# One place modulo 512 bytes for the tiles that TensorE streams, and six operands a pair, not eight, in the inverse transform over k1

## The chip, the cores and the metric

The kernel runs on one core of one Trainium2 chip. The metric is the device time of one execution in microseconds (us); it is given as the median of several executions. Engines are named as in the profile: PE is TensorE's matmul, PEld its weight load, DVE is VectorE, ACT is ScalarE, POOL is GpSimd, SP is SyncE, which here only issues transfers.

## The reference

```python
# attention part, B = 2, S = 12480, D = 128
h_filt = np.maximum(pos_emb @ w1, 0.0) @ w2 * exp(-0.01 * pos)
y = irfft(rfft(x * v, 2 * S) * rfft(h_filt, 2 * S))[:, :S]      # a long convolution per channel
x1 = (x * y).reshape(24960, 128)
# first layer of experts, d_ff = 2048
h = x1 @ w_in
x2 = (h * clip(h + 3, 0, 6) / 6) @ w_out
# second layer
h = maximum(x2 @ w_in2, 0)
out = (h * h) @ w_out2
```

All data are float32. The kernel writes a float32 number as a high and a low part of the type float32r, and makes a product of float32 accuracy from three matmuls of float32r (high by low, low by high, high by high). A matmul whose operands are float32 is made of two instructions.

## The kernel before, in words

**The convolution.** The first stretch makes the filter and, for 32 groups of four channels, the forward transforms, the products and the inverse transform over one of the two indices (`s1`, `s2`, `s3`). `keep` copies what comes out into a staging tile `stg` for a block of 16 channels of both sequences, and `write` sends each of the eight blocks to two tensors in DRAM, `zda` (the first ZA = 4 pairs) and `zdb` (the other 60).

**The pairs.** What is left of the inverse transform is a sum over k1 (K1 = 90 values, real and imaginary part, so 180 rows), for 64 pairs of positions j. `tile_loads` brings for a pair its two halves `za`, `zb`, the table `vt` and the factor `xt`, each with three buffers. `combine` adds and subtracts the two halves to `pp` and `pn` (VectorE for j < 3, then GpSimd). `s4` multiplies: for each of `pp`, `pn` and each of the two sequences two matmuls of 90 rows and 98 (97) columns, one for the real and one for the imaginary part, eight a pair, into one PSUM bank, 390 tokens in all. `gate` multiplies with `xt`, `gate_high` and `gate_low` make the high and the low part `oh`, `ol`.

**The experts.** The 24960 tokens go through both layers in 49 tiles: one of 390 tokens, 47 of 512 and one of 506. A tile of a layer is eight steps. A step is `l1` (two chunks of 128 hidden units, three matmuls each, streaming `oh`, `ol` in layer 1 and `xh`, `xl` in layer 2 into the PSUM tile `ph`), `relu`, `act` and `split` on ScalarE, VectorE and either VectorE or GpSimd (they make `gh` and `gl`), and, LAG = 3 steps later, `l2` (six matmuls that stream `gh`, `gl` into `acc`): 12 matmuls of 512 columns. The weights are `wp0` to `wp3`.

**The order** is written out by hand: what the program issues first on an engine runs first there. The list `tiles` has 15 tiles of layer 1, then one of layer 2 and one of layer 1 in turn, and the rest of layer 2 at the end (AHEAD = 14). The pairs' matmuls are put between those of the steps by `between`, which each step calls at four places:

```python
for f, args, rate in begun.pop(n, ()) if place == 0 else ():
    filling["s4"] = f(*args), rate
if "s4" in filling:
    turn, rate = filling["s4"]
    for _ in range(rate or place % 2):
        if "s4" in filling and next(turn, True):
            del filling["s4"]
```

At rate 2 (19 pairs, those of the first 15 tiles) each place takes two matmuls of a pair, at rate 1 (10 pairs) one, at rate 0 (34 pairs) every second place takes one. What is put in at one place is called a piece below. `gate` and what follows it are planned at the step `done`, and the loads of pair j behind the gate of pair j - 3.

**The start of the experts.** Pair 0 is loaded while the convolution ends, and its last block comes straight from `stg`. Then SP issues `loads(1)`, `loads(2)`, the last `zdb` write and `loads(3)` in this order. A DMA from SP or ACT counts on one of eight semaphores in turn, and waits until the DMA that used the same one before has landed.

Of the kernel before, what the change touches and what calls it, by code (L numbers as in the profile page):

```python
# [37 lines left out]

LEAST = 1.125 * 2.0 ** -15
UOFF = [(0, 98), (98, 98), (196, 97), (293, 97)]  # L40


@with_exitstack
def tile_hyena_moe(ctx: ExitStack, tc, xg, vg, xT, pos, w1d, w2d, fmat, fwin, twc,
                   tws, twcf, twsf, dcs, inv, vtab, w_in1, w_out1, w_in2, w_out2, out):
# [7 lines left out]
    zds = [tc.dram_tile([2, ZA, NBLK, K1, 64], F32, name="zda"),  # L53
           tc.dram_tile([2, 64 - ZA, NBLK, K1, 64], F32, name="zdb")]


    three = cp.tile([128, 1], F32, name="three")


    early = ctx.enter_context(ExitStack())  # L60
# [83 lines left out]
    xv = early.enter_context(tc.tile_pool(name="xv", bufs=3))  # L144
    us = {}
# [113 lines left out]
    def keep(i):  # L259
        g, s = divmod(i, 3)  # L260
        blk, ch0 = g // 4, (g % 4) * 4
        ps = ps3s.pop(i)
        if blk not in stg:
            stg[blk] = sp.tile([128, K1, 2, 2, 16], F32, name=f"stg{blk}", tag="stg")
        nc.scalar.activation(
            stg[blk][:, :, :, s - 1, ch0:ch0 + 4].rearrange("p k r c -> p r c k"),
            ps[:, :, :K4].rearrange("p r (c k) -> p r c k", c=4), AF.Copy)
        if g % 4 == 3 and s == 2:
            sv = stg.pop(blk).rearrange("p k r b c -> p k (r b c)")
            if blk == NBLK - 1:  # L270

                for h, t in enumerate((za, zb)):
                    nc.scalar.dma_start(t.rearrange("k d r b c -> k d (r b c)")[:, blk], sv[64 * h:64 * h + 1])
# [101 lines left out]
    with tc.tile_pool(name="cv_ps", bufs=4, space=PSUM) as vps:  # L375
        def write(blk, z, sv, queue=nc.scalar):
            lo, hi = ((0, ZA), (ZA, 64))[z]
            for h in range(2):
                queue.dma_start(zds[z][h, :, blk], sv[64 * h + lo:64 * h + hi])

        tail, late_rows = [], []
        s1(0)
        twiddle(0)
        s2(1)
        s1(3)
        split1(0)
        twiddle(3)
        s2(2)
        product(1, 0)
        product(1, 1)  # L390
        load(2, 0)
        load(2, 1)
        for i in range(NI + 2):

            a, z = i + AH, i - 2
            if i < NI and i not in (1, 2):
                s2(i)
            if 3 < a < NI:
# [74 lines left out]
    LAG = 3  # L473

    def loads(j):
        za = mo.tile([K1, NBLK, 2, 2, 16], F32, name=f"za{j}", tag="za", bufs=3)
        zb = mo.tile([K1, NBLK, 2, 2, 16], F32, name=f"zb{j}", tag="zb", bufs=3)
        vt[j] = mo.tile([K1, 2, 2, N1], F32, name=f"vt{j}", tag="vt", bufs=3)
        xt[j] = mo.tile([128, TOK], F32, name=f"xt{j}", tag="xt", bufs=3)
        tile_loads(j, za, zb, vt[j], xt[j])  # L480
        zt[j] = (za, zb)

    def combine(j):

        za, zb = zt.pop(j)
        pp = mo.tile([K1, 2, 2, D], F32, name=f"pp{j}", tag="pp")
        pn = mo.tile([K1, 2, 2, D], F32, name=f"pn{j}", tag="pn")
        pm[j] = (pp, pn)

        p, n = (t.rearrange("k r b (d c) -> k d r b c", d=NBLK) for t in (pp, pn))  # L490
        if j == 0:
            for t, z in ((p, za), (n, zb)):
                for r in range(2):
                    nc.scalar.activation(t[:, :, r], z[:, :, r], AF.Copy)
                yield
            return
        for k in range(2):
            for r in range(2):
                eng = nc.vector if j < 3 else nc.gpsimd
                eng.tensor_tensor((p, n)[k][:, :, r], za[:, :, r], zb[:, :, 1 - r],  # L500
                                        (ALU.add, ALU.subtract)[k])
            yield

    py = {}
# [1 line left out]
    def bank(name, k):  # L506
        return mps.tile([128, 512], F32, name=name, tag=f"acc{k % 2}", bufs=1)

    def s4(j, k):

        ps = bank(f"py{j}", k)
        v = vt.pop(j)
        for u in range(4):
            q, b = divmod(u, 2)
            o, n = UOFF[u]
            for r in range(2):
                nc.tensor.matmul(ps[:, o:o + n], pm[j][q][:, r, b, :],  # L517
                                 v[:, q, r, :n], start=(r == 0), stop=(r == 1))
                if u == 3 and r == 1:
                    pm.pop(j)  # L520
                    py[j] = ps
                yield
# [33 lines left out]
    for t in range(1, NTI):  # L556
# [63 lines left out]
    def relu(n):  # L620
        w = size[steps[n][1]]
        r = mo.tile([128, 2, TM], F32, name=f"r{n}", tag="r", bufs=4)
        if steps[n][0] == 0:
            nc.scalar.activation(r[:, :, :w], ph[n][:, :, :w], AF.Relu, bias=three)  # L624
        else:
            nc.scalar.activation(r[:, :, :w], ph[n][:, :, :w], AF.Relu)  # L626
        rs[n] = r
# [72 lines left out]
    for turn in (combine(0), s4(0, 1)):  # L700
        for _ in turn:
            pass
    decode(1, 1)
    decode(2, 1)
    decode(0, 3)
# [45 lines left out]
def _tables():  # L751
# [24 lines left out]
    f = lambda z: np.ascontiguousarray(z, dtype=np.float32)  # L776
    return dict(fmat=f(fmat), fwin=f(fmat * wa), twc=f(twc), tws=f(tws),
                twcf=f(twc * wb[:, None]), twsf=f(tws * wb[:, None]),
                dcs=f(dcs), inv=f(inv), vtab=f(vtab))


def _token_index():
# [59 lines left out]
```

## Time and profile before

| | us |
|---|---|
| median of three runs (2772.34 to 2773.39) | 2772.64 |
| profiled execution, device time | 2773.49 |
| profiled execution, span of the core | 2771.5 |
| TensorE busy | 2728.0 |
| VectorE busy | 1999.9 |
| ScalarE busy | 1932.0 |
| GpSimd busy | 1594.2 |

The profiled execution is 0.85 us over the median. The span falls into three stretches: the convolution (to about 471 us), layer 1 alone with the decoding of layer 2's weights (to about 845 us), and then tiles of both layers in turn, of layer 2 alone at the end. The profile models the end of a matmul: a matmul is listed with its time from first to last element, which overlaps the next one's. What a matmul costs is read from one start to the next.

### The profile page before, as it was taken

What the parts mean: (1) busy time and instruction counts of PE and PEld (TensorE: products, weight loads), DVE (VectorE), ACT (ScalarE), POOL (GpSimd) and SP (SyncE); (2) the same over time, 40 slices, a digit from 0 to 9 for tenths busy, and PEclk for the clock granted to TensorE, in tenths of its full rate; (3) what the DMA queues carried; (4) which work ended last, traced back from release to release, by engine and by line L of the source; (5) the groups of instructions that cost most, each with busy time, mean ns of one, the idle gap of its engine ahead of it and who ended that gap; (6) DMA issues with size and microseconds to landing.
All of it is one profiled execution on the core that took longest, in us unless ns stands there. A gap on an engine that the chain in (4) does not pass through costs nothing.

```text
span 2771.5 us, 33774 instructions
## 1 busy us (share of the span) xinstructions
PE 2728.0 (98%) x12862; PEld 2281.0 (82%) x12862; DVE 1999.9 (72%) x1976; ACT 1932.0 (70%) x2192; POOL 1594.2 (58%) x884
## 2 busy tenths in 40 slices
PE   7999999999999999999999999999999999999999
PEld 6899998788888888888888888888888888888887
DVE  6898998998976666666666666666666666666666
ACT  5445545677777777777777777777777777777776
POOL 3888885576665555555545464645455554444444
PEclk9999999999999999999999999999999999999999
DMA  3253544311111001111010010010111110000000
GB/s 121 80 166 112 146 112 117 99 47 58 40 42 35 18 25 26 27 25 29 25 28 25 21 33 20 24 29 25 29 25 29 25 29 5 8 8 12 12 12 16
DMA packets 136463, 122.28 MB, mean 44 GB/s; under 512 B 99370, under 2 KB 114798, under 8 KB 134894
## 3 DMA queue, kind: packets, MB, share of 16 engines
q1 hardware_dynamic: 127570, 86.27, 11.4%
q10 hardware_dynamic: 8732, 33.85, 4.5%
q8 instruction: 101, 1.65, 0.2%
q14 instruction: 60, 0.49, 0.1%
HBM read 83.68 MB, written 36.37 MB: 43 GB/s over the span
## 4 chain that ended last, share of the span: by engine, by line
PE 89%; DVE 6%; ACT 1%; issue 1%; POOL 0%; DMA 0%; POOLq 0%; ACTq 0%; DVEq 0%
PE ph L616 36%; PE acc L664 36%; PE p L225 7%; PE p L179 4%; PE py L517 3%; PE p L256 3%; DVE r L633 1%; DVE gl L647 1%; ACT gh L643 0%; ACT r L624 0%; DVE ol L542 0%; DVE wm L117 0%; DVE wa L114 0%; DVE wa L125 0%; DVE wa L108 0%
## 5 line engine op out<-in xcount | busy, mean ns | idle before, releaser
L647 POOL TENSOR_TENSOR gl<-r,gh 128x1024 fp32r<-128x1024 f32 (+2 forms) x401 | 966.9, 2411 | 1036.5 <-ACT gh L643 990.4
L664 PE MATMUL acc<-gh,wp 128*128 128x512 f32 (+2 forms) x3136 | 874.8, 399 | 7.5 <-DVE ol L542 7.5
L643 ACT ACTIVATE gh<-r 128x1024 fp32r<-128x1024 f32 (+2 forms) x784 | 820.0, 1046 | 21.1 <-DVE r L633 20.5
L633 DVE SCALAR_TENSOR_TENSOR r<-r,ph 128x1024 f32<-128x1024 f32 (+2 forms) x392 | 475.3, 1213 | 345.6 <-ACT r L624 345.1
L636 DVE SCALAR_TENSOR_TENSOR r<-ph,r 128x1024 f32<-128x1024 f32 (+2 forms) x392 | 477.9, 1219 | 341.9 <-ACT r L626 341.7
L664 PEld LDWEIGHTS acc<-gh,wp 128*128 128x128 f32 x3136 | 575.5, 188 | 123.2 <-PE ph L616 10.4
L624 ACT ACTIVATE r<-ph,three 128x1024 f32<-128x1024 f32 (+2 forms) x392 | 436.1, 1113 | 295.7 <-PE ph L616 290.1
L626 ACT ACTIVATE r<-ph 128x1024 f32<-128x1024 f32 (+2 forms) x392 | 401.8, 1025 | 278.5 <-PE ph L616 278.4
L616 PE MATMUL ph<-oh,wp 128*128 128x512 f32 (+2 forms) x1568 | 571.7, 402 | 0.1
L616 PE MATMUL ph<-xh,wp 128*128 128x512 f32 (+2 forms) x1568 | 554.3, 394 | 0.0
L664 PE MATMUL acc<-gl,wp 128*128 128x512 f32 (+2 forms) x1568 | 484.5, 390 | 1.1 <-POOL gl L647 1.1
L647 DVE TENSOR_TENSOR gl<-r,gh 128x1024 fp32r<-128x1024 f32 (+1 forms) x383 | 473.8, 1237 | 0.0
L664 PEld LDWEIGHTS acc<-gl,wp 128*128 128x128 f32 x1568 | 293.6, 188 | 70.4 <-POOL gl L647 3.3
L616 PEld LDWEIGHTS ph<-xh,wp 128*128 128x128 f32 x1568 | 294.6, 188 | 65.4
L616 PEld LDWEIGHTS ph<-oh,wp 128*128 128x128 f32 x1568 | 296.1, 189 | 56.3 <-ACT oh L536 0.4
L616 PE MATMUL ph<-ol,wp 128*128 128x512 f32 (+2 forms) x784 | 306.2, 391 | 3.7 <-DVE ol L542 3.7
L616 PE MATMUL ph<-xl,wp 128*128 128x512 f32 (+2 forms) x784 | 306.9, 391 | 0.0
L210 ACT ACTIVATE h<-a 128x720 fp32r<-128x720 f32 x96 | 77.3, 806 | 194.0 <-DVE a L198 163.4
L211 POOL TENSOR_TENSOR l<-a,h 128x720 fp32r<-128x720 f32 x96 | 168.2, 1752 | 65.0 <-ACT h L210 65.0
L616 PEld LDWEIGHTS ph<-xl,wp 128*128 128x128 f32 x784 | 147.3, 188 | 31.6
L616 PEld LDWEIGHTS ph<-ol,wp 128*128 128x128 f32 x784 | 148.2, 189 | 28.8 <-DVE ol L542 4.8
L500 POOL TENSOR_TENSOR pp<-za,zb 90x256 f32<-90x256 f32 x122 | 135.2, 1128 | 37.8 <-PE ph L616 37.8
(97 smaller groups left out, 2697.1 us busy)
## 6 DMA issues: line engine op xcount, KB each, us to landing
zdb<-stg ACTq DMA_DIRECT2D x14, 1350.0 KB
x<-xg SPq DMA_DIRECT2D x64, 196.0 KB
v<-vg SPq DMA_DIRECT2D x64, 196.0 KB
xt<-xT SPq DMA_DIRECT2D x63, 195.0 KB
out<-ot ACTq DMA_DIRECT2D x47, 256.0 KB
za<-zdb SPq DMA_DIRECT2D x60, 180.0 KB
zb<-zdb SPq DMA_DIRECT2D x60, 180.0 KB
vt<-vtab SPq DMA_DIRECT2D x63, 137.8 KB
```

The costliest lines, as they stand in the source:

```text
L179: nc.tensor.matmul(ps[:, c // 2, o:o + 2 * K1], src, fm if s else fw)
L211: nc.gpsimd.tensor_tensor(l, gt, h.bitcast(F32), ALU.subtract)
L225: nc.tensor.matmul(pv, wt, x, start=(n == 0), stop=(n == len(ops) - 1))
L500: eng.tensor_tensor((p, n)[k][:, :, r], za[:, :, r], zb[:, :, 1 - r], (ALU.add, ALU.subtract)[k])
L616: nc.tensor.matmul(ps[:, c, :w], wt, x[:, :w], start=(m == 0), stop=(m == 2))
L624: nc.scalar.activation(r[:, :, :w], ph[n][:, :, :w], AF.Relu, bias=three)
L626: nc.scalar.activation(r[:, :, :w], ph[n][:, :, :w], AF.Relu)
L633: nc.vector.scalar_tensor_tensor(g, g, 6.0, pv, ALU.min, ALU.mult)
L636: nc.vector.scalar_tensor_tensor(g, pv, 0.0, g, ALU.max, ALU.mult)
L643: nc.scalar.activation(h, g, AF.Copy)
L647: eng.tensor_tensor(l, g, h.bitcast(F32), ALU.subtract)
L664: nc.tensor.matmul(ps, wt, x, start=(q == 0 and m == 0), stop=(q == NP - 1 and m == len(ops) - 1))
```

## The change: what it does

**The operands of the transform.** The 180 rows (real and imaginary part of 90 values) become one axis of 2 * K1 rows in DRAM, with 32 numbers a row and block. 128 of them are the full operand, one for each sequence; the other KR = 52 rows of both sequences lie under each other as one operand of 104 rows. Its table `vr` has zeros where a sequence meets the other's columns, so one matmul of 194 or 196 columns serves both. A pair has four matmuls of 128 rows and two of 104. The second half is loaded with its two parts swapped, so that one addition and one subtraction make each operand. Pair 0 keeps its eight matmuls (`s4_first`).

**The loads.** A pair has ten DMAs where it had four, the tables now behind the z loads:

```diff
-    def tile_loads(j, za, zb, v, x):
-        nc.sync.dma_start(v, vtab[j])
-        nc.sync.dma_start(x, xT[j])
-        nb = NBLK - (j == 0)
-        for h, t in enumerate((za, zb)):
-            zr = zds[0][h, j] if j < ZA else zds[1][h, j - ZA]
-            nc.sync.dma_start(t.rearrange("k d r b c -> k d (r b c)")[:, :nb],
-                              zr[:nb].rearrange("d k c -> k d c"))
+    def tile_loads(j, zs, v, x):
+        for h in range(2):
+            zr = rows_of(h, j).rearrange("d k c -> k d c")
+            full, rest = zs[h]
+            if h == 0:
+                nc.sync.dma_start(full, zr[:128])
+            else:
+                nc.sync.dma_start(full[:K1], zr[K1:])
+                nc.sync.dma_start(full[K1:], zr[:128 - K1])
+            first = 128 if h == 0 else 128 - K1
+            for b in range(2):
+                nc.sync.dma_start(rest[KR * b:KR * b + KR],
+                                  zr[first:first + KR, :, 16 * b:16 * b + 16])
+        nc.sync.dma_start(v[0], vtab1[j])
+        nc.sync.dma_start(v[1], vtab2[j])
         nc.sync.dma_start(x, xT[j])
...
-        for u in range(4):
-            q, b = divmod(u, 2)
-            o, n = UOFF[u]
-            for r in range(2):
-                nc.tensor.matmul(ps[:, o:o + n], pm[j][q][:, r, b, :],
-                                 v[:, q, r, :n], start=(r == 0), stop=(r == 1))
+        for q in range(2):
+            full, rest = pm[j][q]
+            o, n = UOFF[2 * q]
+            nc.tensor.matmul(ps[:, o:o + 2 * n], rest, vr[:, q, :2 * n], start=True, stop=False)
+            yield
+            for b in range(2):
+                o, n = UOFF[2 * q + b]
+                nc.tensor.matmul(ps[:, o:o + n], full[:, b, :], vf[:, q, :n],
+                                 start=False, stop=b == 1)
...
-            done = n + (4, 2, 1)[rate]
+            done = n + (3, 2, 1)[rate]
```

**The addresses.** The small tile `three` leaves its place at the left end of SBUF and becomes 88 numbers wide at the right end. So everything that is allocated from the left lies 32 bytes lower, and everything from the right 352 bytes lower:

```diff
-    three = cp.tile([128, 1], F32, name="three")
+    bp = ctx.enter_context(tc.tile_pool(name="bias", bufs=1, side="right"))
+    three = bp.tile([128, 88], F32, name="three")
```

| tiles (every buffer of each) | address modulo 512 before | after |
|---|---|---|
| `wp0` to `wp3` | 160 | 128 |
| `oh`, `ol`, `gh`, `gl` | 160 | 128 |
| `xh`, `xl` | 480 | 128 |
| `vt` (before) | 160, 192, 224 | |
| `vf`, `vr` (after) | | 128, 416, 192 and 480, 0, 32 |

**What it does to the order.** On PE, in the tile of layer 1 in which a pair is spread out at rate 0, there stand before (`ph` is `l1`, `acc` is `l2`, `py` the transform):

```order
L517 MATMUL py_12617<-vt_12004,pp_12460 128x98
L664 MATMUL acc_28_12585<-gh_12572,wp_4191 128x512 x4
L664 MATMUL acc_28_12585<-gl_12573,wp_4191 128x512 x2
L517 MATMUL py_12617<-vt_12004,pp_12460 128x98
L616 MATMUL ph_12633<-oh_11977,wp_85 128x512
L616 MATMUL ph_12633<-ol_11978,wp_85 128x512
L616 MATMUL ph_12633<-oh_11977,wp_85 128x512 x2
L616 MATMUL ph_12633<-ol_11978,wp_85 128x512
L616 MATMUL ph_12633<-oh_11977,wp_85 128x512
L517 MATMUL py_12617<-vt_12004,pp_12460 128x98
```

and for the same pair after the change, with `vr`, `pr` the wide operand of 104 rows and `vf`, `pf` the full one:

```order
L552 MATMUL py_12994<-vr_12335,pr_12829 128x196
L703 MATMUL acc_28_12953<-gh_12940,wp_4196 128x512 x4
L703 MATMUL acc_28_12953<-gl_12941,wp_4196 128x512 x2
L556 MATMUL py_12994<-vf_12334,pf_12828 128x98
L655 MATMUL ph_13010<-oh_12305,wp_88 128x512
L655 MATMUL ph_13010<-ol_12306,wp_88 128x512
L655 MATMUL ph_13010<-oh_12305,wp_88 128x512 x2
L655 MATMUL ph_13010<-ol_12306,wp_88 128x512
L655 MATMUL ph_13010<-oh_12305,wp_88 128x512
L556 MATMUL py_12994<-vf_12334,pf_12828 128x98
```

The pieces stand at the same places, the first of each three is the wide one, and a pair ends after three steps, not four.

On SP, at the start of the experts, there stand before, for pairs 1 and 2 and the last write of `zdb`:

```order
L136 DMA vt_4326<-vtab 90x392
L137 DMA xt_4327<-xT 128x390
L141 DMA za_4324<-zda 90x8x64
L141 DMA zb_4325<-zda 90x8x64
L136 DMA vt_4334<-vtab 90x392
L137 DMA xt_4335<-xT 128x390
L141 DMA za_4332<-zda 90x8x64
L141 DMA zb_4333<-zda 90x8x64
L379 DMA zdb<-stg_4008 60x5760 x2
```

and after the change, for pair 1 alone, ahead of the same ten for pair 2 and only then the write:

```order
L153 DMA z0f_4331<-zda 128x8x32
L159 DMA z0r_4332<-zda 52x8x16 x2
L155 DMA z1f_4333<-zda 90x8x32
L156 DMA z1f_4333<-zda 38x8x32
L159 DMA z1r_4334<-zda 52x8x16 x2
L161 DMA vf_4335<-vtab 128x196
L162 DMA vr_4336<-vtab 104x392
L163 DMA xt_4337<-xT 128x390
```

The write moves from behind eight DMAs to behind twenty, and the tables of pair 1 from ahead of the z loads to behind them.

## Rows read from the trace of the kernel before

**Rows 1.** The page: span, busy times, and the chain that ended last by engine.

```profile
span 2771.5 us, 33774 instructions
...
PE 2728.0 (98%) x12862; PEld 2281.0 (82%) x12862; DVE 1999.9 (72%) x1976; ACT 1932.0 (70%) x2192; POOL 1594.2 (58%) x884
...
PE 89%; DVE 6%; ACT 1%; issue 1%; POOL 0%; DMA 0%; POOLq 0%; ACTq 0%; DVEq 0%
```

**Rows 2.** Timeline of PE, first matmul of tiles; columns start us, us, what.

```profile
1497.88 0.48 PE L616 MATMUL ph<-xh,wp 128*128 128x512 f32 x1
...
1520.15 0.40 PE L616 MATMUL ph<-oh,wp 128*128 128x512 f32 x1
...
1543.87 0.48 PE L616 MATMUL ph<-xh,wp 128*128 128x512 f32 x1
...
2451.81 0.40 PE L616 MATMUL ph<-xh,wp 128*128 128x512 f32 x1
...
2651.49 0.40 PE L616 MATMUL ph<-xh,wp 128*128 128x512 f32 x1
```

**Rows 3.** Timeline, first matmul of steps in both layers, and who makes `gl`.

```profile
1506.29 0.40 PE L616 MATMUL ph<-xh,wp 128*128 128x512 f32 x1
...
1507.20 2.41 POOL L647 TENSOR_TENSOR gl<-r,gh 128x1024 fp32r<-128x1024 f32 x1 [3.14 <-ACT gh L643]
...
1509.06 0.40 PE L616 MATMUL ph<-xh,wp 128*128 128x512 f32 x1
...
1510.13 1.22 DVE L647 TENSOR_TENSOR gl<-r,gh 128x1024 fp32r<-128x1024 f32 x1
...
1511.83 0.40 PE L616 MATMUL ph<-xh,wp 128*128 128x512 f32 x1
...
1522.89 0.39 PE L616 MATMUL ph<-oh,wp 128*128 128x512 f32 x1
...
1531.06 0.39 PE L616 MATMUL ph<-oh,wp 128*128 128x512 f32 x1
```

**Rows 4.** Timeline of PE, pieces of the transform: two a step, and two matmuls each.

```profile
509.71 0.58 PE L517 MATMUL py<-vt,pp 90*128 90x98 f32 x4
...
513.13 0.58 PE L517 MATMUL py<-vt,pn 90*128 90x97 f32 x4
...
1531.28 0.39 PE L616 MATMUL ph<-ol,wp 128*128 128x512 f32 x1
...
1534.49 0.39 PE L616 MATMUL ph<-ol,wp 128*128 128x512 f32 x1
```

**Rows 5.** Float32 matmuls of 180 columns: timeline, then groups (busy us, mean ns).

```profile
447.85 1.38 PE L179 MATMUL p<-fm,v 98*128 98x180 f32 x8
...
L179 PE MATMUL p<-fm,v 98*128 98x180 f32 x512 | 88.6, 316 | 1.6 <-DVE a L198 1.0 <-POOL v L156 0.5
```

**Rows 6.** Windows: length, busy us of PE, PEld, DVE, ACT, POOL, clock, DMA, GB/s.

```profile
471.00:845.00 374.00, 363.90 (x1746) 305.05 (x1744) 329.18 (x314) 275.11 (x316) 233.87 (x140) 0.99 0.24 60
...
477.00:485.00 8.00, 6.91 (x28) 6.91 (x29) 7.75 (x14) 4.78 (x8) 0.00 (x0) 0.57 1.01 268
```

**Rows 7.** Timeline, start of the experts, and SP's DMA queue (packets, MB, share).

```profile
474.32 0.33 SPq L141 DMA_DIRECT2D zb<-zda  x1
...
476.73 0.96 SPq L379 DMA_DIRECT2D zdb<-stg  x2
...
477.62 0.75 DVE L500 TENSOR_TENSOR pp<-za,zb 90x256 f32<-90x256 f32 x2
...
478.09 1.17 PE L517 MATMUL py<-vt,pp 90*128 90x98 f32 x4 [3.21 <-DVE pp L500]
...
495.08 0.65 SPq L80 DMA_DIRECT2D wr<-w_in  x1
...
509.89 0.66 ACT L104 ACTIVATE wm<-wr 128x512 f32<-128x512 f32 x1
...
q1 hardware_dynamic: 127570, 86.27, 11.4%
```

More of the change, by code (lines that the diff above doesn't have):

```diff
@@ L40 @@
 UOFF = [(0, 98), (98, 98), (196, 97), (293, 97)]
+KR = 2 * K1 - 128
 @with_exitstack
 def tile_hyena_moe(ctx: ExitStack, tc, xg, vg, xT, pos, w1d, w2d, fmat, fwin, twc,
-                   tws, twcf, twsf, dcs, inv, vtab, w_in1, w_out1, w_in2, w_out2, out):
+                   tws, twcf, twsf, dcs, inv, vtab0, vtab1, vtab2, w_in1, w_out1, w_in2, w_out2, out):
     nc = tc.nc
@@ L50, in tile_hyena_moe @@
     hp = ctx.enter_context(tc.tile_pool(name="hfilt", bufs=1))
-    zds = [tc.dram_tile([2, ZA, NBLK, K1, 64], F32, name="zda"),
-           tc.dram_tile([2, 64 - ZA, NBLK, K1, 64], F32, name="zdb")]
-    three = cp.tile([128, 1], F32, name="three")
+    zds = [tc.dram_tile([2, ZA, NBLK, 2 * K1, 32], F32, name="zda"),
+           tc.dram_tile([2, 64 - ZA, NBLK, 2 * K1, 32], F32, name="zdb")]
+    bp = ctx.enter_context(tc.tile_pool(name="bias", bufs=1, side="right"))
+    three = bp.tile([128, 88], F32, name="three")
     early = ctx.enter_context(ExitStack())
@@ L132, in decode, with rows_of, first_loads @@
             next(parts[part], None)
-    def tile_loads(j, za, zb, v, x):
-        nc.sync.dma_start(v, vtab[j])
-        nc.sync.dma_start(x, xT[j])
-        nb = NBLK - (j == 0)
-        for h, t in enumerate((za, zb)):
-            zr = zds[0][h, j] if j < ZA else zds[1][h, j - ZA]
-            nc.sync.dma_start(t.rearrange("k d r b c -> k d (r b c)")[:, :nb],
-                              zr[:nb].rearrange("d k c -> k d c"))
+    def rows_of(h, j):
+        return zds[0][h, j] if j < ZA else zds[1][h, j - ZA]
+    def first_loads(za, zb, v, x):
+        nc.sync.dma_start(v, vtab0)
+        nc.sync.dma_start(x, xT[0])
+        for h, t in enumerate((za, zb)):
+            zr = rows_of(h, 0)[:NBLK - 1].rearrange("d (r k) c -> k d r c", r=2)
+            for r in range(2):
+                nc.sync.dma_start(t[:, :NBLK - 1, r], zr[:, :, r])
+    def tile_loads(j, zs, v, x):
[13 more added lines that the diff above has]
+        nc.sync.dma_start(v[1], vtab2[j])
+        nc.sync.dma_start(x, xT[j])
     xv = early.enter_context(tc.tile_pool(name="xv", bufs=3))
@@ L263, in keep @@
         if blk not in stg:
-            stg[blk] = sp.tile([128, K1, 2, 2, 16], F32, name=f"stg{blk}", tag="stg")
+            stg[blk] = sp.tile([128, 2, K1, 2, 16], F32, name=f"stg{blk}", tag="stg")
         nc.scalar.activation(
-            stg[blk][:, :, :, s - 1, ch0:ch0 + 4].rearrange("p k r c -> p r c k"),
+            stg[blk][:, :, :, s - 1, ch0:ch0 + 4].rearrange("p r k c -> p r c k"),
             ps[:, :, :K4].rearrange("p r (c k) -> p r c k", c=4), AF.Copy)
         if g % 4 == 3 and s == 2:
-            sv = stg.pop(blk).rearrange("p k r b c -> p k (r b c)")
+            sv = stg.pop(blk).rearrange("p r k b c -> p (r k) (b c)")
             if blk == NBLK - 1:
                 for h, t in enumerate((za, zb)):
-                    nc.scalar.dma_start(t.rearrange("k d r b c -> k d (r b c)")[:, blk], sv[64 * h:64 * h + 1])
+                    for r, queue in enumerate((nc.scalar, nc.sync)):
+                        queue.dma_start(t[:, blk, r], sv[64 * h:64 * h + 1, K1 * r:K1 * r + K1])
                 tail.append(sv)
@@ L475, in loads @@
     def loads(j):
-        za = mo.tile([K1, NBLK, 2, 2, 16], F32, name=f"za{j}", tag="za", bufs=3)
-        zb = mo.tile([K1, NBLK, 2, 2, 16], F32, name=f"zb{j}", tag="zb", bufs=3)
-        vt[j] = mo.tile([K1, 2, 2, N1], F32, name=f"vt{j}", tag="vt", bufs=3)
-        xt[j] = mo.tile([128, TOK], F32, name=f"xt{j}", tag="xt", bufs=3)
-        tile_loads(j, za, zb, vt[j], xt[j])
-        zt[j] = (za, zb)
-    def combine(j):
[L485 to L492, printed above, removed]
-                for r in range(2):
[L494 to L501, printed above, removed]
+        zt[j] = [(mo.tile([128, NBLK, 32], F32, name=f"z{h}f{j}", tag=f"z{h}f", bufs=3),
+                  mo.tile([2 * KR, NBLK, 16], F32, name=f"z{h}r{j}", tag=f"z{h}r", bufs=3))
+                 for h in range(2)]
@@ new lines, in loads, with combine_first @@
+        vt[j] = (mo.tile([128, 2, N1], F32, name=f"vf{j}", tag="vf", bufs=3),
+                 mo.tile([2 * KR, 2, 2 * N1], F32, name=f"vr{j}", tag="vr", bufs=3))
+        xt[j] = mo.tile([128, TOK], F32, name=f"xt{j}", tag="xt", bufs=3)
+        tile_loads(j, zt[j], vt[j], xt[j])
+    def combine_first():
+        both = op.tile([128, 2, TM], F32, name="pm0", tag="gl")
+        pm[0] = [both[:K1, q].rearrange("k (r b c) -> k r b c", r=2, b=2) for q in range(2)]
+        for t, z in zip(pm[0], zt.pop(0)):
+            t = t.rearrange("k r b (d c) -> k d r b c", d=NBLK)
+            z = z.rearrange("k d r (b c) -> k d r b c", b=2)
+            for r in range(2):
+                nc.scalar.activation(t[:, :, r], z[:, :, r], AF.Copy)
@@ new lines, in combine @@
+    def combine(j):
+        zs = zt.pop(j)
+        pm[j] = [(mo.tile([128, 2, D], F32, name=f"pf{q}{j}", tag=f"pf{q}"),
+                  mo.tile([2 * KR, D], F32, name=f"pr{q}{j}", tag=f"pr{q}")) for q in range(2)]
+        eng = nc.vector if j < 3 else nc.gpsimd
+        for q in range(2):
+            sign = (ALU.add, ALU.subtract)[q]
+            full, rest = pm[j][q]
+            (fa, ra), (fb, rb) = (
+                (f.rearrange("k d (b c) -> k d b c", b=2), r) for f, r in zs)
+            eng.tensor_tensor(full.rearrange("k b (d c) -> k d b c", d=NBLK), fa, fb, sign)
+            eng.tensor_tensor(rest.rearrange("k (d c) -> k d c", d=NBLK), ra, rb, sign)
@@ L516, in s4 @@
             for r in range(2):
-                nc.tensor.matmul(ps[:, o:o + n], pm[j][q][:, r, b, :],
+                nc.tensor.matmul(py[0][:, o:o + n], p[q][:, r, b, :],
                                  v[:, q, r, :n], start=(r == 0), stop=(r == 1))
-                if u == 3 and r == 1:
+    def s4(j, k):
+        ps = bank(f"py{j}", k)
+        vf, vr = vt.pop(j)
+        for q in range(2):
+            full, rest = pm[j][q]
+            o, n = UOFF[2 * q]
[5 more added lines that the diff above has]
+                                 start=False, stop=b == 1)
+                if q == 1 and b == 1:
                     pm.pop(j)
@@ L623, in relu @@
         if steps[n][0] == 0:
-            nc.scalar.activation(r[:, :, :w], ph[n][:, :, :w], AF.Relu, bias=three)
+            nc.scalar.activation(r[:, :, :w], ph[n][:, :, :w], AF.Relu, bias=three[:, :1])
         else:
@@ L699, in tile_hyena_moe @@
     decode(0, 1)
-    for turn in (combine(0), s4(0, 1)):
-        for _ in turn:
-            pass
+    combine_first()
+    s4_first(1)
     decode(1, 1)
@@ L771, in _tables @@
     vtab = np.stack([np.cos(ph), -np.sin(ph)], axis=3) * (2.0 / n)
+    rows = vtab.transpose(0, 3, 1, 2, 4).reshape(NT, 2 * K1, 2, N1)
+    vtab2 = np.zeros((NT, 2 * KR, 2, 2 * N1))
+    for q in range(2):
+        w = UOFF[2 * q][1]
+        for b in range(2):
+            vtab2[:, KR * b:KR * b + KR, q, w * b:w * b + w] = rows[:, 128:, q, :w]
     wa = np.exp(-0.01 * 128 * n1).astype(np.float32).astype(np.float64)[:, None]
@@ L778, in _tables @@
                 twcf=f(twc * wb[:, None]), twsf=f(tws * wb[:, None]),
-                dcs=f(dcs), inv=f(inv), vtab=f(vtab))
+                dcs=f(dcs), inv=f(inv), vtab0=f(vtab[0]), vtab1=f(rows[:, :128]), vtab2=f(vtab2))
 def _token_index():
```

12 lines of the change are left out of this document (6 added, 6 removed).

## The prediction

> **What bounds the kernel now.** I read the page's busy times and its chain first [rows 1]. TensorE is busy for 98% of the span, and the chain of work that ended last is TensorE for 89%, VectorE for 6% and nothing else above 1%: the kernel is as long as its matmuls take, one behind the other, plus a few waits on VectorE. GpSimd, which does most of the sums that the change touches, has 0% of the chain. So the change is priced by what it does to the distance from one matmul's start to the next, not by the instructions it saves elsewhere. The profiled execution took 2773.49 us with a span of 2771.5; the sum below is made against 2773.49, and the median of the runs is 0.85 lower.
>
> The next view is the timeline of TensorE, read at the first matmul of each tile [rows 2]. A layer-2 tile between layer-1 tiles takes 1520.15 - 1497.88 = 22.27 us. In the tail, where only layer 2 is left, nine tiles take 2651.49 - 2451.81 = 199.68 us, 22.19 each. A layer-1 tile with one pair of the inverse transform takes 1543.87 - 1520.15 = 23.72.
>
> Then the first matmul of each step (12 matmuls of 512 columns) [rows 3]. A layer-2 step takes 2.77 us (1506.29 to 1509.06, and again to 1511.83). Three layer-1 steps without a piece of the transform take 1531.06 - 1522.89 = 8.17 us, 2.72 each. The counts, shapes and clock are the same; 2.77 against 2.72 is 231 ns a matmul against 227. The two layer-2 steps are alike although GpSimd makes the low part `gl` in the first (1507.20) and VectorE in the second (1510.13): what the other engines do at the time does not set the distance. The first layer-1 step behind a layer-2 tile is in between, 1522.89 - 1520.15 = 2.74. What differs, by the table of addresses in the section on the change, is the place of the streamed tile: in layer 1 every streamed tile and every weight lies at 160 modulo 512, in layer 2 `xh` and `xl` lie at 480 while `gh`, `gl` and the weights stay at 160, and each step goes from one place to the other and back.
>
> **Term 1, one place modulo 512.** After the change all of them lie at 128. If a stream that never changes its place runs at 2.72 us a step, a layer-2 tile takes 8 x 2.72 = 21.76 us. The 33 full tiles between layer-1 tiles then gain 22.27 - 21.76 = 0.51 each, 16.8 us, and the 14 full tiles of the tail 0.43 each, 6.0. The 34 first layer-1 steps gain 0.02 each, 0.7. Together -23.5 us; I take -23. The bounds are 0 (the place is not the cause) and -23.5, unless 128 is itself another place than 160, which no row shows; that is two of the rivals.
>
> [...]
>
> **Term 2, six operands, not eight.** The columns that pass through the array stay the same, 8 x 97.5 = 780 before and 4 x 97.5 + 2 x 195 = 780 after, each as two instructions since the operands are float32. So by columns nothing is won. But the short ones do not cost their columns. In a layer-1 tile the second matmul of two neighbouring steps with two pieces in between starts at 1531.28 and 1534.49 [rows 4]: 3.21 us, against 2.72, so a piece of one short matmul costs (3.21 - 2.72)/2 = 0.245 us; the whole tile says the same, (23.72 - 21.76)/8 = 0.245. In the first stretch, where a piece holds two of them, three matmuls and a piece take (513.13 - 509.71)/3 = 1.14 us, less 3 x 0.227 is 0.46 a piece: the second one costs 0.215. Two instructions of 98 columns cost 0.215 to 0.245, 0.11 each or more, and longer float32 instructions are the yardstick: 180 columns follow each other at (1.38 - 0.316)/7 = 0.152 us [rows 5], which is 0.84 ns a column with nothing on top. So a short one (98 x 0.84 = 0.083) waits for something that a long one hides, and 195 columns are past that point: 195 x 0.84 = 0.165 an instruction, 0.33 a matmul, 0.35 with what is left of a piece's own start (0.245 - 0.215 = 0.03, less a little).
>
> A pair that is spread out (44 of 63) goes from 8 x 0.245 = 1.96 to 4 x 0.245 + 2 x 0.35 = 1.68: -0.28 each, -12.3. Bounds: if the extra over 0.83 ns a column is a fixed price of each matmul (0.245 - 0.165 = 0.08), a long one costs 0.33 + 0.08 = 0.41 and the gain is 0.16 each, -7.0; if the long one costs its columns alone, -0.32, -14.1. I take -12, nearer to the rows of 180 columns because 195 is next to them. A pair in the first stretch (19) goes from 4 x 0.46 = 1.84 to three pieces, 2 x (0.35 + 0.215) + 0.46 = 1.59: -0.25, -4.7. But there VectorE is busy for 329.18 of 374 us [rows 6] and TensorE waits for it now and then, so I let half of that through: -2.4, bounds 0 and -4.7. More partitions per operand (128 and 104, not 90) cost nothing as long as only columns count; a 98-row operand is what the yardstick has.
>
> **Term 3, the start of the experts.** Ten loads a pair take the place of four on SyncE's queue, and most are of 64- and 128-byte pieces: 2048 + 1664 = 3712 packets of z a pair, not 1440. Once the stream runs three pairs are loaded ahead (a pair has 390/512 of a tile, 23.72 x 0.76 = 18 us), and even at the queue's mean of 0.114 x 16 x 2771.5 us / 127570 packets = 39.6 ns a packet [rows 7], 3712/16 x 39.6 ns = 9.2 us fit; that costs nothing there, and would cost up to 9 us a pair if it didn't. At the start there is no lead. SyncE can load the second z only when block 7 has landed (474.32), VectorE's sum starts at 477.62, and TensorE has waited 3.21 us for it at 478.09 [rows 7]. After the change four z loads stand there where one stood, 0.33 to 0.48 us apart [rows 7], and the tables `vf`, `vr` come behind them, not ahead: 3 x 0.4 + 2 x 0.4 = 2.0 us later at most, 1.2 at least. Behind VectorE's wait stand the decoding and the first activations. The write of `zdb` (476.73) stands behind 20 loads, not 8: 12 x 0.45 = 5.4 us later, and behind it the raw weights of layer 2 (495.08), which ScalarE first reads at 509.89; of 14.8 us, most is needed for 2 MB, so 0 to 6 us more wait. [...] Sum of the term: 0 to +10, I take +4.
>
> [...]
>
> Nothing else moves TensorE: GpSimd's sums get fewer and longer off the chain, the copies of `keep` write with another stride on ScalarE, which has 1% of the chain, and all tables of the convolution move by the same 32 bytes.
>
> **Sum.** 2773.5 - 23 - 12 - 2.4 + 4 = 2740.1 for a profiled execution, 2739 as a median.
>
> **Rivals.**
> *The place does nothing.* Layer-2 steps stay at 2.77 because of something else that goes with the layer. For it: ScalarE's and VectorE's instructions change form at the same step. Against it: the step does not change with the engine that makes `gl`, and the first layer-1 step is half way. Time: 2740.1 + 23 - 0.85 = 2762.
>
> *128 is a worse place than 160 (slower).* All streamed tiles share a place, but layer 1 also goes to 2.77. 49 layer-1 tiles x 8 steps x 0.05 = +20 us and no gain in layer 2: 2773.5 + 20 - 14.4 + 4 = 2783, 2782 as a median. It decides from 14.4 - 4 = 10.4 us on, that is from 0.027 us a layer-1 step. Against it: the rows know 160 alone as a common place, and nothing in them makes 160 special.
>
> *The start costs much more.* Loads at the start hold VectorE and ScalarE for 15 us and not 4: 2750. For it: [rows 7], where the queue is already what TensorE waits for.
>
> *More than that.* 128 is a better place than 160, by 1 ns a matmul or more in 9400: under 2730.
>
> **Chances.** The forecast (2728 to 2750) 0.69; the costly start (2750 to 2761) 0.09; the place does nothing (2757 to 2767) 0.12; slower 0.05; more gain (under 2728) 0.05. The range 2728 to 2761 holds the first two and a part of the third, 0.8. A measurement of this kernel can tell about 0.2%, 5.5 us, from no change. Faster by more than that (under 2767): 0.92; within: 0.03; slower: 0.05.
>
> **What would show it.** Term 1: layer-2 tiles of 21.8 us in the timeline, a tail of 14 tiles 6 us shorter, layer-1 steps still 2.72. Term 2: one-pair layer-1 tiles of 23.45 with three steps that hold pieces, not four. Term 3: TensorE's wait for the sum of pair 1 longer by 1 to 2 us, and the first layer-2 tile no more than 4 us nearer to the first pair than the pairs' gain says. The prediction is wrong if layer-2 steps stay at 2.77, or if layer-1 steps leave 2.72.

## The result, and the profile after

The changed kernel takes 2742.81 us (median of 4 executions, 2740.78 to 2743.84) against 2772.87 us before in the same session (4 executions, 2772.34 to 2773.39): a ratio of 0.9891, 95% interval 0.9874 to 0.9908. The forecast was 2739 with a range of 2728 to 2761. The profiled execution took 2743.84 us, 29.65 less than the one of before (2773.49).

The page of the changed kernel, whose span is 2742.1 us (busy time of each engine; the chain that ended last), which answers to [rows 1]:

```profile
PE 2692.3 (98%) x12610; PEld 2266.5 (83%) x12610; DVE 1990.1 (73%) x1976; ACT 1933.0 (70%) x2192; POOL 1560.1 (57%) x884
...
PE 87%; DVE 6%; ACT 1%; issue 1%; SPq 1%; DMA 0%; POOL 0%; POOLq 0%; ACTq 0%; DVEq 0%
```

TensorE is still 98% busy and still the chain, with 252 matmul instructions fewer. SP's queue, which was not in the chain before, now holds 1% of it. That is the first hint of where part of the gain is given back.

The timeline of PE after the change (start us, us, what), at the first matmul of steps and tiles, and at the `l2` matmuls of one step, answers to [rows 2, 3]:

```profile
1490.07 0.39 PE L655 MATMUL ph<-xh,wp 128*128 128x512 f32 x1
...
1491.43 1.07 PE L703 MATMUL acc<-gh,wp 128*128 128x512 f32 x4
1492.34 0.61 PE L703 MATMUL acc<-gl,wp 128*128 128x512 f32 x2
1492.79 0.39 PE L655 MATMUL ph<-xh,wp 128*128 128x512 f32 x1
...
1511.83 0.39 PE L655 MATMUL ph<-oh,wp 128*128 128x512 f32 x1
...
1535.33 0.39 PE L655 MATMUL ph<-xh,wp 128*128 128x512 f32 x1
...
2428.06 0.39 PE L655 MATMUL ph<-xh,wp 128*128 128x512 f32 x1
...
2623.90 0.39 PE L655 MATMUL ph<-xh,wp 128*128 128x512 f32 x1
```

A layer-2 step takes 1492.79 - 1490.07 = 2.72 us, not 2.77. A layer-2 tile takes 1511.83 - 1490.07 = 21.76, not 22.27; nine tiles of the tail take 195.84, 21.76 each, not 22.19. A layer-1 tile with one pair takes 1535.33 - 1511.83 = 23.50, not 23.72.

The same view at two pieces of that layer-1 tile, a wide one and a short one, answers to [rows 4]:

```profile
1528.56 0.63 PE L703 MATMUL acc<-gl,wp 128*128 128x512 f32 x2
1529.03 0.49 PE L552 MATMUL py<-vr,pr 104*128 104x194 f32 x2
...
1529.59 0.39 PE L655 MATMUL ph<-ol,wp 128*128 128x512 f32 x1
...
1531.90 0.62 PE L703 MATMUL acc<-gl,wp 128*128 128x512 f32 x2
1532.36 0.36 PE L556 MATMUL py<-vf,pf 128*128 128x97 f32 x2
...
1532.81 0.39 PE L655 MATMUL ph<-ol,wp 128*128 128x512 f32 x1
```

From the first `acc` to `ol` there are three long matmuls (two of `gl` and one of `oh`, 0.227 each, 0.68) and the piece: 1.03 - 0.68 = 0.35 us for the wide one, 0.91 - 0.68 = 0.23 for the short one.

At the start of the experts it went the other way. The timeline of all engines after the change, which answers to [rows 7]:

```profile
481.12 0.92 PE L552 MATMUL py<-vr,pr 104*128 104x196 f32 x2 [5.02 <-DMA vr<-vtab]
...
485.41 0.87 SPq L401 DMA_DIRECT2D zdb<-stg  x2
...
511.11 0.37 SPq L82 DMA_DIRECT2D wr<-w_in  x1
...
520.13 0.67 ACT L106 ACTIVATE wm<-wr 128x512 f32<-128x512 f32 x1 [8.23 <-DMA wr<-w_in]
...
523.35 2.08 PE L703 MATMUL acc<-gh,wp 128*128 128x512 f32 x4 [3.82 <-ACT gh L682]
...
605.10 0.39 PE L655 MATMUL ph<-oh,wp 128*128 128x512 f32 x1
...
848.18 0.34 PE L655 MATMUL ph<-xh,wp 128*128 128x390 f32 x1
```

TensorE waits 5.02 us at the first pair, not 3.21, and it now waits for the table `vr`, which is issued (at 478.25) behind seven loads of z and the table `vf`; VectorE had the sum `pr` ready at 479.66. The write of `zdb` leaves 8.7 us later, the raw weights `wr` 16.0 us later (495.08 before). ScalarE waits 8.23 us for them, and TensorE 3.82 us for the `gh` that stands behind that in ScalarE's order. The sixth tile begins at 605.10 and the first layer-2 tile at 848.18. The same two in the timeline of before:

```profile
599.56 0.39 PE L616 MATMUL ph<-oh,wp 128*128 128x512 f32 x1
...
844.94 0.42 PE L616 MATMUL ph<-xh,wp 128*128 128x390 f32 x1
```

The difference by stretch: the start loses 605.10 - 599.56 = 5.5 us; the ten tiles from there to the first layer-2 tile win 245.38 - 243.08 = 2.3; the 33 layer-2 tiles between layer-1 tiles win 33 x 0.51 = 16.8; the tail wins 14 x 0.43 = 6.0; the layer-1 tiles among them win 0.22 in each of 23 with one pair and 0.48 in each of 10 with two (medians of the timeline), 9.9. Together 29.5 of the 29.65.

### The profile page after: what moved, and what is told of

Same layout as the page of the kernel before. It is cut to its first block, busy times and chain, and to the rows that moved or that the text cites. A ratio compares the mean times of both kernels' runs of the same rounds, so it can differ in the third digit from the quotient of the medians.

```text
span 2742.1 us, 33813 instructions
## 1 busy us (share of the span) xinstructions
PE 2692.3 (98%) x12610; PEld 2266.5 (83%) x12610; DVE 1990.1 (73%) x1976; ACT 1933.0 (70%) x2192; POOL 1560.1 (57%) x884
## 4 chain that ended last, share of the span: by engine, by line
PE 87%; DVE 6%; ACT 1%; issue 1%; SPq 1%; DMA 0%; POOL 0%; POOLq 0%; ACTq 0%; DVEq 0%
PE ph L655 36%; PE acc L703 36%; PE p L246 7%; PE p L200 4%; PE p L277 3%; PE py L556 2%; PE py L552 1%; DVE r L672 1%; DVE gl L686 1%; ACT r L663 1%; SPq L159 0%; DVE wa L110 0%; DVE ol L581 0%; DVE wp L129 0%; DVE wa L116 0%
## 5 line engine op out<-in xcount | busy, mean ns | idle before, releaser
L703 PE MATMUL acc<-gh,wp 128*128 128x512 f32 (+2 forms) x3136 | 861.5, 395 | 11.5 <-DVE ol L581 7.7
L655 PE MATMUL ph<-xh,wp 128*128 128x512 f32 (+2 forms) x1568 | 544.9, 388 | 0.0
L527 POOL TENSOR_TENSOR pr<-z0r,z1r 104x128 f32<-104x128 f32 x122 | 147.7, 1211 | 0.3 <-DVE r L672 0.3
```

The source lines that it names most:

```text
L527: eng.tensor_tensor(rest.rearrange("k (d c) -> k d c", d=NBLK), ra, rb, sign)
L655: nc.tensor.matmul(ps[:, c, :w], wt, x[:, :w], start=(m == 0), stop=(m == 2))
L703: nc.tensor.matmul(ps, wt, x, start=(q == 0 and m == 0), stop=(q == NP - 1 and m == len(ops) - 1))
```

## The experiments

The theory: the place of the streamed tiles sets the distance between long matmuls (term 1), the number of short float32 instructions sets what a pair costs (term 2), and the start is dearer by its queue (term 3). The rivals: the place does nothing; 128 is a special place; short matmuls cost by their columns; the start is dear by the clock.

### Each half of the change alone

The place alone is the kernel before with the edit to `three` that the section on the change shows (and `bias=three[:, :1]`), and nothing else.

> The kernel before with the one edit to the addresses (all streamed tiles and weights at 128 modulo 512), the eight operands and the loads as before. Theory (one place for all streams): layer-2 tiles take 21.76 us and not 22.27 or 22.19, layer-1 tiles with one pair 23.70, the start as before; 2749.5 us, 23 less than before. Rival (the address does nothing and the operands or the later times of other engines made layer 2 faster): layer-2 tiles 22.27, 2772.6 us.

It took 2752.98 us (2751.02 to 2754.9, 4 runs), before 2772.25 in the same session, ratio 0.993 (0.9915 to 0.9945): -19.3 us. Its timeline of PE:

```profile
1492.03 0.36 PE L518 MATMUL py<-vt,pn 90*128 90x97 f32 x2
1492.17 0.48 PE L617 MATMUL ph<-xh,wp 128*128 128x512 f32 x1
1492.49 0.40 PE L617 MATMUL ph<-xl,wp 128*128 128x512 f32 x1
...
1495.04 0.39 PE L617 MATMUL ph<-xh,wp 128*128 128x512 f32 x1
...
1497.76 0.39 PE L617 MATMUL ph<-xh,wp 128*128 128x512 f32 x1
...
1514.08 0.39 PE L617 MATMUL ph<-oh,wp 128*128 128x512 f32 x1
```

The steps are at 2.72 with nothing changed but addresses, so the rival "the place does nothing" falls. But the tile takes 1514.08 - 1492.17 = 21.91 here (median of all 21.88) and not 21.76. The first three rows show why: the eighth piece of the pair stands right ahead of the tile's first matmul, and the second one follows only 0.32 us later, not 0.227. A part of that piece, about 0.12 us in the median, is counted in the layer-2 tile. So the place gives 33 x 0.39 + 14 x 0.43 + 0.7 = 19.6 us.

The operands alone are the changed kernel with `three` back in its old place (so `xh`, `xl` at 480 and the rest at 160):

```diff
-    bp = ctx.enter_context(tc.tile_pool(name="bias", bufs=1, side="right"))
-    three = bp.tile([128, 88], F32, name="three")
+    three = cp.tile([128, 1], F32, name="three")
```

> The changed kernel with the small tile back at its old place, so weights, oh, ol, gh, gl at 160 and xh, xl at 480 modulo 512. Theory: layer-2 tiles go back to 22.27 and 22.19 us, layer-1 tiles with one pair 23.51, the dearer start of the changed kernel stays; 2766 us, 23 more than the changed kernel and 7 less than before. Rival (layer 2 got faster by the operands): 2743 us.

It took 2763.28 us (2760.89 to 2764.6, 5 runs), ratio 0.9965 (0.9951 to 0.998): -9.0 us. Its timeline:

```profile
1495.51 0.40 PE L654 MATMUL ph<-xh,wp 128*128 128x512 f32 x1
...
1498.29 0.40 PE L654 MATMUL ph<-xh,wp 128*128 128x512 f32 x1
...
1517.70 0.40 PE L654 MATMUL ph<-oh,wp 128*128 128x512 f32 x1
...
1541.22 0.40 PE L654 MATMUL ph<-xh,wp 128*128 128x512 f32 x1
```

Steps of 2.78 (2.773 in the median) and layer-2 tiles of 22.19, exactly the tail's value: the spilled piece is gone, since a pair now ends after three steps, and only the place is left. The layer-1 tile is at 23.52. The two halves, -19.3 and -9.0, add up to -28.3 of about -30. Most of the gap is the spilled piece: it takes 22.27 - 22.19 = 0.08 us of a layer-2 tile at the old places and 0.12 at the common one, and 33 x 0.04 = 1.3 us are won by neither half alone.

### Which place

All at 160, the changed kernel with `three` at the left again and a tile of 80 numbers at the right end:

```diff
-    bp = ctx.enter_context(tc.tile_pool(name="bias", bufs=1, side="right"))
-    three = bp.tile([128, 88], F32, name="three")
+    three = cp.tile([128, 1], F32, name="three")
+    bp = ctx.enter_context(tc.tile_pool(name="bias", bufs=1, side="right"))
+    pad = bp.tile([128, 80], F32, name="pad")
+    nc.gpsimd.memset(pad, 0.0)
```

> The changed kernel with everything at 160 modulo 512: weights, oh, ol, gh, gl, xh, xl. Theory (what counts is that the place is common): layer-2 steps 2.72 us, layer-2 tiles 21.76, 2743 us as the changed kernel. Rival (128 is a good place, as a multiple of 64 or 128): layer-2 steps over 2.72 us, up to 2.77, and up to 2765 us.

One execution took 2741.64 us, with layer-2 steps of 2.72 (in its timeline 1487.81 to 1490.53). 128 is no better and no worse than 160. The next kernel puts the streams together at 448 and leaves the weights at 128, by a tile of 80 numbers at the left and one of 8 at the right:

> The changed kernel with all streamed tiles at 448 modulo 512 and the weights left at 128. Theory A (a stream must keep its own place from one matmul to the next): steps of both layers 2.72 us, 2743 us. Theory B (the stream must lie at the place of the weights that are loaded beside it): no step is at 2.72 any more, 2.77 in both layers, 784 x 0.05 = 39 us more, 2782 us.

One execution took 2765.65 us, which neither theory had forecast: 23 us more than the changed kernel although all streams share a place. Between layer-1 tiles, 22 of its layer-2 tiles took 21.97 us and 11 took 22.40; its layer-1 tiles with one pair took 23.64 in the median. So the weights' place counts too. Three more kernels move the tiles by other distances: the first two only make `three` narrower (72 and 24 numbers, not 88), the third has 16 numbers at the left and 72 at the right.

`xh`, `xl` 64 bytes from all the rest:

> The changed kernel with the layer-2 stream xh and xl at 192 modulo 512, all else at 128 (64 bytes from its weights and from the layer-1 stream). Theory A, any place other than the common one costs the same: a layer-2 step takes 2.77 us again, 564 layer-2 tiles' steps gain 0.053 each, about 2764 us. Theory C, the distance between the stream and the weights sets the step in units of 0.027 us: the step is one of 2.72, 2.747, 2.773, and the time lies at about 2742, 2752 or 2764.

`xh`, `xl` 256 bytes from all the rest:

> The same with xh and xl at 384, 256 bytes from the weights. Theory A: a layer-2 step of 2.77 us and about 2764 us. Theory C: another of the three steps than at 64 bytes may come out; if 256 is a place like 0, 2.72 us and 2742 us.

All streams 64 bytes from the weights:

> The changed kernel with all streams together at 192 and the weights left at 128. The run with the streams at 448 took 2765.7 us with steps of 2.747. Theory A2, streams need only agree with one another and 448 was bad by its distance: at 64 bytes 2742 us. Theory C, every distance other than 0 costs: steps of 2.747 to 2.773 and 2760 to 2770 us.

One execution each: 2765.01, 2744.52 and 2765.55 us. The timelines of PE, first `xh` 64 bytes off, then 256 bytes off, then all streams 64 bytes from the weights (in a tile between layer-1 tiles, and in the tail):

```profile
1499.19 0.40 PE L655 MATMUL ph<-xh,wp 128*128 128x512 f32 x1
...
1500.58 1.10 PE L703 MATMUL acc<-gh,wp 128*128 128x512 f32 x4
1501.51 0.62 PE L703 MATMUL acc<-gl,wp 128*128 128x512 f32 x2
1501.96 0.40 PE L655 MATMUL ph<-xh,wp 128*128 128x512 f32 x1
```

```profile
1493.40 0.39 PE L655 MATMUL ph<-xh,wp 128*128 128x512 f32 x1
...
1496.12 0.39 PE L655 MATMUL ph<-xh,wp 128*128 128x512 f32 x1
```

```profile
1500.89 0.40 PE L658 MATMUL ph<-xh,wp 128*128 128x512 f32 x1
...
1503.69 0.40 PE L658 MATMUL ph<-xh,wp 128*128 128x512 f32 x1
...
2490.74 0.40 PE L658 MATMUL ph<-xh,wp 128*128 128x512 f32 x1
...
2493.49 0.40 PE L658 MATMUL ph<-xh,wp 128*128 128x512 f32 x1
```

2.77 at 64 bytes, 2.72 at 256 bytes, and 2.75 to 2.80 where all streams lie 64 bytes from the weights. "Any place other than the common one costs the same" and "every distance other than 0 costs" fall with the second of them, "streams need only agree with one another" with the third. With the places of before (480 and 160, 320 apart) and of the run at 448 and 128 (320 apart), all seven layouts agree with one rule: a distance of 0 or 256 is free (2.72 us a step), one of 64 or 320, which are the same modulo 256, costs 0.03 to 0.08 us a step. Other distances were not tried.

The rule is one of layouts, and not of the single matmul. With `xh`, `xl` 64 bytes off, `gh` still lies at the place of its weights, and yet its four matmuls take 1501.51 - 1500.58 = 0.93 us, against 1492.34 - 1491.43 = 0.91 in the changed kernel; the six of `xh` and `xl` take 1.39 against 1.36. So about half of what the step loses falls on matmuls whose own distance is 0. Where in turn all 12 matmuls of a step lie 64 bytes from their weights, most steps lose less (2.75) than where only six of them do (2.77). What TensorE loses the time by, and why a step costs 2.77 in one case of 64 bytes and 2.75 or 2.80 in another, stays open. The tiles of layer 2 that lie in one pool with `xh` and `xl` (what layer 1 hands on, and `ot`) move with them in these kernels; TensorE reads neither, but no run moves `xh` and `xl` without them.

### What a short matmul costs

The changed kernel with only the first 49 columns of its four 128-row matmuls a pair; the other columns of these products are left out:

```diff
             for b in range(2):
                 o, n = UOFF[2 * q + b]
+                n = 49
                 nc.tensor.matmul(ps[:, o:o + n], full[:, b, :], vf[:, q, :n],
                                  start=False, stop=b == 1)
```

> The changed kernel with 49 instead of 98 (or 97) columns in the four 128-row matmuls of a pair; the other columns of these products are left out. Theory, a float32 matmul this short costs what its issue and weight load cost, not its columns: the short piece stays at 0.235 us and the time at about 2743 us. Rival, a fixed price and then columns: a short piece loses 2 x 49 columns at about 0.84 ns, 0.08 us, and 252 such pieces make about 20 us, so about 2723 us.

One execution took 2743.43 us. Its timeline of PE at a short piece, and the ends of a layer-1 tile:

```profile
1511.29 0.39 PE L656 MATMUL ph<-oh,wp 128*128 128x512 f32 x1
...
1524.79 0.62 PE L704 MATMUL acc<-gl,wp 128*128 128x512 f32 x2
1525.25 0.32 PE L557 MATMUL py<-vf,pf 128*128 128x49 f32 x2
...
1525.71 0.40 PE L656 MATMUL ph<-ol,wp 128*128 128x512 f32 x1
...
1534.79 0.39 PE L656 MATMUL ph<-xh,wp 128*128 128x512 f32 x1
```

The piece takes 0.92 - 0.68 = 0.24 us and the tile 23.50, as with twice the columns. The rival "a fixed price and then columns" (2723) falls: with 49 columns and with 98 a short float32 matmul here costs its two instructions, 0.12 us each, and the columns between change nothing. Each instruction has a weight load of 128 columns beside it in both kernels (504 loads for the 504 instructions of the `vf` matmuls in the changed one); no run changes that, so the weight load as the cause is neither shown nor excluded.

### The start of the experts

Four kernels change only the order in which SP issues transfers, or the queue that issues them. The first plans the ten loads of pair 4 behind the raw weights:

```diff
-                plan(late_do, gated[j - 3] + 1, loads, j)
+                plan(late_do, 7 if j == 4 else gated[j - 3] + 1, loads, j)
```

> The changed kernel with the 20 loads of step 4 planned behind the raw weights of the second expert instead of ahead of them. Theory, the raw weights come late because SP's queue of loads stands still behind the write of zdb: ScalarE's wait of 8.2 us for wr and TensorE's stall of 4.2 us for gh go, and the first layer-2 tile begins 3 to 6 us earlier than at 848.2; about 2738 us. Rival, the start is dear by the throttled clock alone: the stall moves, the time stays at 2742 to 2744 us.

One execution took 2741.83 us. The edit moves the loads of pair 4 alone, which are ten, not the 20 that the expectation speaks of. In its timeline the raw weights leave 7.0 us earlier and ScalarE reads them without a wait:

```profile
481.71 0.99 PE L552 MATMUL py<-vr,pr 104*128 104x196 f32 x2 [5.41 <-DMA vr<-vtab]
...
504.12 0.36 SPq L82 DMA_DIRECT2D wr<-w_in  x1
...
516.41 0.67 ACT L106 ACTIVATE wm<-wr 128x512 f32<-128x512 f32 x1
```

The stall is gone, and yet the first layer-2 tile begins at 846.23, only 2.0 us earlier. The windows of 485 to 501 us show where the rest went (length, busy us of PE, PEld, DVE, ACT, POOL, granted clock, DMA share, GB/s): first the changed kernel, then this one.

```profile
485.00:501.00 16.00, 13.08 (x76) 12.24 (x74) 15.52 (x27) 9.70 (x15) 0.00 (x0) 1.00 0.88 214
```

```profile
485.00:501.00 16.00, 13.91 (x59) 13.45 (x58) 13.40 (x22) 6.66 (x10) 0.00 (x0) 0.71 0.90 213
```

76 matmuls at a granted clock of 1.00 against 59 at 0.71 (0.80 from 485 to 493 us, 0.63 from 493 to 501), behind the wait of 5.41 us at the first pair that this kernel still has. So both theories were half right: the stall was the queue's, and 17 matmuls fewer, 17 x 0.227 = 3.9 us, took most of it back in this one execution.

The second puts the narrow loads of pairs 1 to 3 on POOL's queue:

```diff
-                nc.sync.dma_start(rest[KR * b:KR * b + KR],
+                (nc.gpsimd if j < 4 else nc.sync).dma_start(rest[KR * b:KR * b + KR],
```

> The changed kernel with the loads of the narrow inverse operands of steps 1 to 3 put on GpSimd's queue, not SP's. Theory, the number of transfers on SP's queue delays what stands behind them: 12 transfers fewer there, the zdb write leaves 3 us or more earlier, the raw weights about 5 us earlier; 2738 to 2740 us. Rival, it is the write of zdb itself that all wait for: no change, or slower by GpSimd's issue time; 2743 to 2746 us.

One execution took 2737.76 us. The write of `zdb` left at 482.41 and `wr` at 504.80, 3.0 and 6.3 us earlier than in the changed kernel; ScalarE's wait for `wr` fell to 3.12 us, and TensorE's at the first pair to 3.67. The number of transfers on the queue counts here, as the theory said.

The third has the first edit and, for every pair, the tables ahead of the z loads:

```diff
     def tile_loads(j, zs, v, x):
+        nc.sync.dma_start(v[0], vtab1[j])
+        nc.sync.dma_start(v[1], vtab2[j])
+        nc.sync.dma_start(x, xT[j])
         for h in range(2):
...
-        nc.sync.dma_start(v[0], vtab1[j])
-        nc.sync.dma_start(v[1], vtab2[j])
-        nc.sync.dma_start(x, xT[j])
```

> raw_first and, in each step's loads, the two tables and the gate's rows ahead of the eight loads of z. Theory: TensorE's wait for vr at the first pair falls from 5.0 to about the 3.2 us of before, on top of raw_first; about 2736 us, ratio to before 0.987, faster than both kernels. Rival, another wait follows at once (z's products): as raw_first, 2738 us.

It took 2736.22 us (2735.01 to 2736.97, 4 runs) against 2772.91 before in the same session: ratio 0.9868 (0.9851 to 0.9884). Against the changed kernel's 2742.81 that is 6.6 us less, and the two sets of runs, of two sessions, don't overlap. Its timeline and window:

```profile
477.67 0.60 PE L552 MATMUL py<-vr,pr 104*128 104x196 f32 x2 [3.71 <-DVE pr L527]
...
500.89 1.52 SPq L82 DMA_DIRECT2D wr<-w_in  x1
...
509.69 0.68 ACT L106 ACTIVATE wm<-wr 128x512 f32<-128x512 f32 x1
...
839.41 0.34 PE L655 MATMUL ph<-xh,wp 128*128 128x390 f32 x1
```

```profile
485.00:501.00 16.00, 14.07 (x77) 13.01 (x76) 15.05 (x24) 9.71 (x15) 0.00 (x0) 0.98 0.78 179
```

TensorE waits 3.71 us at the first pair, for VectorE's sum again as in [rows 7], and is granted 0.98 from 485 to 501 us. It is the fastest version here. Of the 8.8 us by which its first layer-2 tile lies ahead of the changed kernel's, 1.7 stand already at the first matmul of the experts (470.39 against 472.09). That start lies between 470.4 and 472.3 in all profiled executions, so 1 to 2 us between two single executions can come from there.

The fourth has all three edits:

> best_a with pool_queue. If the queue's length matters, 1 to 3 us less than best_a, about 2734 us; if not, the same as best_a or more by up to 2 us.

2737.48 us (2735.64 to 2738.78, 4 runs), ratio 0.9871 (0.9856 to 0.9886): no better than without POOL's queue, and not the 1 to 3 us less that it would be if the queue's length still mattered. The raw weights leave 3.6 us earlier (497.26), but in the third kernel ScalarE already reads them without a wait.

## Why the prediction was right, and where its sizes were off

**The place (term 1): right in cause, too large.** Forecast -23, measured -19.6 by the tiles and -19.3 by the medians. The steps of layer 2 went to 2.72 as forecast, and the layer-1 steps without a piece stayed there. The condition that the prediction put ("a stream that never changes its place") is not enough, though: with all streams at 448 and the weights at 128 no stream changes its place, and the steps take 2.75 and 2.80. The term came out because the change moves the weights with the streams. What failed is the step "the 33 full tiles between layer-1 tiles then gain 22.27 - 21.76 = 0.51 each": 0.12 of it was the pair's last piece that reaches into the tile, 33 x 0.12 = 3.9 us, which belongs to term 2. The rows of before had the sign of it, 0.08 of it: 22.27 in [rows 2] against 22.19 in the tail, and 8 x 2.77 is 22.16. The place alone changed a step from 2.77 to 2.72, so the measurement decides against the lower bound of 0; whether TensorE waits for another reader of SBUF, or for itself, no run shows.

**The operands (term 2): right.** Forecast -12, measured 3.9 + 9.9 - 0.7 = 13.1 us less behind the place, where 0.7 is the place's part in layer-1 tiles. In the run of the operands alone it is 33 x 0.08 + 9.2 = 11.8, with 9.2 from the layer-1 tiles. The one-pair tile came out at 23.50 and not at 23.45, since part of the pair's gain lies in the tile behind it. The wide piece was forecast at 0.35 and measured at 0.35; the short one at 0.245 and 0.23 to 0.24. That "a short one waits for something that a long one hides" was an inference; the run with 49 columns shows that columns are not what it pays for. What it waits for, if it waits, is not shown.

**The first stretch and the start (-2.4 and term 3, +4): together +1.6 forecast, +3.2 measured.** The ten tiles behind the start won 2.3 us. The start lost 5.5, pairs' gain included. The waits were named rightly and sized too low: TensorE's wait grew by 1.81 us, within the 1.2 to 2.0, but it ended with `vr` and not with the sum; the write of `zdb` left 8.7 us later, not 5.4; and the raw weights 16.0 us later with an 8.23 us wait of ScalarE, where 0 to 6 were allowed. The step that failed is that it counted the transfers ahead of the write and not those between the write and the raw weights: `wr` follows the write by 18.4 us in the kernel before (eight loads between) and by 18.8 in the one with the loads of pair 4 behind (ten), but by 22.4 in the one with POOL's queue (sixteen) and by 25.7 in the changed one (twenty). In the one with all three edits, with six between, it is still 19.3, so the first 18 to 19 us do not come from the number of loads. In the changed kernel the raw weights needed 9.0 us (511.11 to 520.13). So 5.8 of the 14.8 us of before were slack: the 5.4 us of the forecast would have fitted in, 16.0 did not. The upper end of term 3, +10, holds more than the waits of 2.0 and 6 us; no run shows that rest, and the granted clock was 0.76 from 471 to 485 us and 1.00 from 485 to 501 us both before and after. The rival of a much costlier start (15 us) didn't come.

The three differences, +3.4, -1.1 and +1.6, make 3.9; the profiled execution is 3.7 over the sum of 2740.1.

## What to carry to other kernels

Read the distance between the starts of like matmuls in each layer or stage; where it differs by a per cent or two with the same shapes and clock, look at the addresses of the streams and the weights and move a small tile until they agree (here a step took 2.72 us at a distance of 0 or 256 bytes and 2.75 to 2.80 at one of 64 or 320). Between long matmuls count short float32 matmuls (here 0.23 to 0.24 us each with 49 and with 98 columns; one of 195 cost 0.35, half as much again) by their number and not by their columns, and charge one that stands at a boundary to one side only. When a load is cut into more transfers, follow the whole queue behind it to its last urgent transfer, and issue ahead of the pieces the small tables that the waiting engine needs with them.

## What was not expected of the hardware

The steps come in levels 0.027 us apart: 2.720 us for 12 matmuls in the changed kernel, 2.747 and 2.800 with all streams 64 bytes from the weights, 2.773 with the operands alone; what TensorE does differs between these kernels in nothing but addresses. 256 bytes is as good as no distance (2744.52 against 2742.81 us), though 64 bytes costs 22 us (2765.01). A matmul of 49 columns costs as much as one of 98 (a tile of 23.50 us with either).

The granted clock behind the first pair's wait is not the same in each execution of the same start. The kernel with 49 columns issues the same there as the changed kernel and waits 4.98 us, not 5.02, yet it is granted 0.71 from 485 to 501 us where the changed kernel is granted 1.00. Its first layer-2 tile begins at 847.53 all the same, against 848.18, as ScalarE then waits 4.32 us for the raw weights and not 8.23: what the lower clock took there, that shorter wait gave back.
